# One order of one core's work set anew: fp32r groups, first loads on two queues, ScalarE's table early

## The chip, the cores and the metric

The kernel runs on one core of a Trainium2 chip. The metric is device time in microseconds. Engines: PE is TensorE, PEld its weight load, DVE VectorE, ACT ScalarE, POOL GpSimd, SP SyncE (here it only issues DMAs; SPq and ACTq are the queues of SyncE and ScalarE).

## The reference

Attention with random features (8 batches, 8 heads, 576 positions, head size 64, 128 features), whose output, 4608 tokens of 512, goes through two matrix products with a GELU between them.

```python
scale = 1.0 / np.sqrt(np.sqrt(D))
def phi(x):
    proj = np.einsum('bhsd,md->bhsm', x, omega)
    h = proj - np.sum(x * x, axis=-1, keepdims=True) / 2.0
    h = h - np.max(h, axis=-1, keepdims=True)
    return np.exp(h) / np.sqrt(m)
kv = np.einsum('bhsm,bhsd->bhmd', k_p, v)
z = np.sum(k_p, axis=2)
num = np.einsum('bhsm,bhmd->bhsd', q_p, kv)
den = np.einsum('bhsm,bhm->bhs', q_p, z)[..., None] + 1e-06
...
h = x @ w_in                                   # 512 -> 2048
g = 0.5 * h * (1.0 + erf(h * inv_sqrt2))
return g @ w_out                               # 2048 -> 512
```

## The kernel before

A unit is two heads of one batch; there are 32. Of each unit TensorE projects keys and queries on omega, ScalarE takes exponentials, TensorE multiplies keys by values (`kv`, line 769), turns the queries (`q_trans`, 798), multiplies them by the result (`num_plain`, 806) and turns the quotient back (`back`, 832). Units 0 to 7 ("plain") project in fp32, in `pair` (737: sixteen matmuls for each of keys and queries) and `shared` (744: the 64 positions at the edge that two heads share). Their maxima are `top` (749, VectorE), their exponentials `exp_tiles` (753, ScalarE). Units 8 to 31 ("split") copy their inputs to fp32r in a high and a low part (931, 936) and project them in groups of fp32r matmuls: `proj` (944, two or one of 256 columns for keys) and `proj_q` (966, two of 288 for queries).

The tokens form 18 blocks of 256. Block 0 goes through both products in fp32 (1203, 1257). The others are split in two f16 parts and use one level of a Strassen-like scheme for the first product (`sw1` and `sw2`, line 1216, 128 columns), GELU on ScalarE, and for the second product `mm2` (1264 to 1266, 512 columns). The weights come in 16 pieces of two DMAs of 512 KB (`w_load`, 545): eight of w_in first, then eight of w_out. Each is converted by ScalarE (`w_hi` 550, `w_lo` 555), VectorE (`w_shift` 558, `w_max` 567) and GpSimd (`w_round` 564); two buffers hold the pieces. When all of w_in is through, its largest value sets a scale, which TensorE helps to find (615, 621).

Nothing is scheduled by hand at the place where it is written. Each step is an `op` with an engine, a cost in microseconds, and the keys it reads and writes. A planner (`Planner.run`) walks through time with these costs: at every moment it gives each free engine, among the steps that are ready by its own account, the one with the lowest rank, and writes the instructions out in that order. `RANK` holds one number for each step, in the order in which the steps are made; for each engine the numbers are 0, 1, 2, ... without a gap, so a rank is a place on its engine. The costs reach the chip only through the order, and through filler matmuls (1421) where the planner sees TensorE idle for over 0.9 us. Two extra costs are known to it on TensorE: 0.057 us (`psw`) where a group tagged 'r' (fp32r) comes behind a step without a tag, and 0.3 where a 't' group comes behind another kind. The matmuls of both products have no tag. ScalarE pays 1.28 (`tsw`) when its table changes between exponential and GELU.

At the start SyncE issues omega (two DMAs to the two halves of the partitions, `load_om`, 508), then the first weight piece, the keys of unit 1, the queries of units 0 and 1, the second weight piece, the values of units 1 and 0. The keys of unit 0 go out on ScalarE's queue (`load_two`, 722; `load_v`, 718 for values). TensorE runs 17 warm-up matmuls (504). ScalarE's first step is `w_hi` of the first piece.

Of the kernel before, what the change touches and what calls it, by code (L numbers as in the profile page):

```python
# [8 lines left out]
F32 = mybir.dt.float32  # L9
# [26 lines left out]
RANK = (0, 3, 1, 0, 0, 4, 1, 4, 8, 0, 1, 1, 2, 2, 2, 5, 0, 5, 8, 3, 9, 4, 8, 12, 5, 23, 2, 6, 10, 11, 14, 7, 6, 15, 25, 18, 26, 22, 35, 25, 25, 3, 5,  # L36
# [187 lines left out]
class Planner:  # L224
# [45 lines left out]
    def run(self, lat, hop, alloc, put):  # L270
        for o in self.ops:
            o.due = RANK[o.id]
            o.left, o.ready, o.end, o.out = len(o.deps) + len(o.after), 0.0, None, False
        free, cand = {e: 0.0 for e in ('PE', 'ACT', 'DVE', 'POOL', 'SP')}, {e: [] for e in ('PE', 'ACT', 'DVE', 'POOL', 'SP')}
        self.tab, self.ptab, self.dma, now, n = None, None, 0.0, 0.0, 0
        port = {'DVE': 0.0, 'POOL': 0.0}

# [1182 lines left out]
```

## Time and profile before

| | |
|---|---|
| three runs | 942.03, 943.58 (median), 944.38 us |
| the profiled execution | 943.64 us |
| its span, first to last instruction | 941.5 us |
| TensorE busy | 925.3 us |
| VectorE busy | 748.5 us |
| ScalarE busy | 736.4 us |
| GpSimd busy | 486.8 us |

Times in a trace count from the span's start. The end of a matmul in the records is modelled: matmuls that follow one another overlap, so their cost is read from start to start, not from their durations. What stands under "idle before" is the time that an engine was empty ahead of an instruction, with the one that released it.

### The profile page before, as it was taken

The numbers are of one execution on the slowest core, as the hardware profiler recorded it, in microseconds if no ns is written. First come the engines' busy times: TensorE is split into PE (matmuls) and PEld (weight loads), VectorE is DVE, ScalarE is ACT, GpSimd is POOL, SyncE is SP. The second block draws the span as 40 slices with busy tenths as digits, with TensorE's granted clock in tenths as the row PEclk, the third lists the DMA queues.
The fourth block names the chain that finished last, engine by engine and source line by source line (L and its number), as shares of the span: only waits on it lengthen the run. The fifth ranks groups of instructions, "written<-read, shape, count | busy, mean of one in ns | idle before, by whom it ended". The sixth has DMA issues, their size and how long they took to land.

```text
span 941.5 us, 25835 instructions
## 1 busy us (share of the span) xinstructions
PE 925.3 (98%) x10041; PEld 702.6 (75%) x10041; DVE 748.5 (80%) x2086; ACT 736.4 (78%) x1615; POOL 486.8 (52%) x717
## 2 busy tenths in 40 slices
PE   7999999999999999999999999999999999999998
PEld 6996777777767777777777767777776777776776
DVE  3868898999999988879988999898788997643332
ACT  5998978889999787889779789977889886644343
POOL 1354655856778474775446667664657751400000
PEclk8999999999999999999999999999999999999999
DMA  8786324122422131221221332112122200000000
GB/s 241 229 248 200 115 52 133 35 80 69 117 60 88 41 99 56 63 66 56 68 80 41 88 91 77 51 53 63 52 75 63 63 2 24 13 14 23 1 24 24
DMA packets 46314, 71.46 MB, mean 76 GB/s; under 512 B 13680, under 2 KB 22256, under 8 KB 46192
## 3 DMA queue, kind: packets, MB, share of 16 engines
q1 hardware_dynamic: 46048, 69.51, 24.9%
q8 instruction: 79, 1.29, 0.6%
q14 instruction: 43, 0.35, 0.1%
q10 hardware_dynamic: 144, 0.29, 0.1%
HBM read 60.36 MB, written 9.44 MB: 74 GB/s over the span
## 4 chain that ended last, share of the span: by engine, by line
PE 82%; DVE 7%; ACT 4%; POOL 3%; DMA 2%; issue 2%; SPq 1%; POOLq 0%; ACTq 0%
PE h L1216 30%; PE acc L1264 10%; PE acc L1266 10%; PE acc L1265 10%; PE acc L1257 3%; PE at L944 2%; PE at L966 2%; PE h L1203 2%; PE at L1029 2%; PE at L816 2%; PE at L832 1%; PE h L769 1%; DMA vt<-in_v 1%; PE at L806 1%; POOL ts L1185 1%
## 5 line engine op out<-in xcount | busy, mean ns | idle before, releaser
L936 POOL TENSOR_TENSOR r<-xt,r 64x288 fp32r<-64x288 f32 (+2 forms) x216 | 165.8, 780 | 126.6 <-ACT r L931 81.2
L1216 PE MATMUL h<-xh,w 128*128 128x128 f16 x2176 | 217.4, 219 | 0.0
L1264 PE MATMUL acc<-woh,gh 128*128 128x512 f16 (+1 forms) x544 | 205.2, 377 | 0.0
L1265 PE MATMUL acc<-woh,gl 128*128 128x512 f16 (+1 forms) x544 | 204.5, 376 | 0.7 <-DVE gl L1254 0.7
L1266 PE MATMUL acc<-wol,gh 128*128 128x512 f16 (+1 forms) x544 | 204.5, 376 | 0.0
L1216 PE MATMUL h<-xl,w 128*128 128x128 f16 x1088 | 199.0, 219 | 0.0
L1216 PEld LDWEIGHTS <-w 128*128 128x128 f16 x3264 | 195.7, 98 | 4.2 <-issue 0.6
L1216 PE MATMUL h<-xh,wih 128*128 128x128 f16 x816 | 157.4, 220 | 2.7 <-DVE h L1234 1.5
L1216 PE MATMUL h<-xl,wih 128*128 128x128 f16 x816 | 156.6, 219 | 0.0
L1216 PE MATMUL h<-xh,wil 128*128 128x128 f16 x816 | 156.6, 219 | 0.0
L1254 DVE SCALAR_TENSOR_TENSOR gl<-h,bs,gh 128x512 f16<-128x512 f32 x136 | 101.0, 744 | 67.1 <-ACT gh L1251 66.3
L1216 PEld LDWEIGHTS <-wih 128*128 128x128 f16 x1632 | 139.9, 98 | 15.9 <-DVE h L1234 2.2
L1242 ACT ACTIVATE h<-h,bs 128x512 f32<-128x512 f32 x136 | 90.0, 662 | 61.8 <-PE h L1216 56.5
L1251 ACT ACTIVATE gh<-h,bs 128x512 f16<-128x512 f32 x136 | 93.5, 689 | 14.6 <-PE acc L1266 11.8
L1266 PEld LDWEIGHTS <-gh 128*128 128x128 f16 x560 | 54.7, 98 | 62.5
L931 ACT CAST r<-xt 128x256 fp32r<-128x256 f32 (+2 forms) x216 | 83.6, 408 | 14.3 <-PE at L966 9.4
L1216 PEld LDWEIGHTS <-wil 128*128 128x128 f16 x816 | 80.0, 98 | 12.0 <-issue 2.4
L1264 PEld LDWEIGHTS <-gh 128*128 128x128 f16 x560 | 54.7, 98 | 43.1
L1265 PEld LDWEIGHTS <-gl 128*128 128x128 f16 x560 | 54.9, 98 | 40.4 <-DVE gl L1254 1.0
L1223 ACT COPY g<-h 128x256 f32<-128x256 f32 x136 | 50.4, 371 | 35.1 <-PE h L1216 33.8
L1229 DVE TENSOR_TENSOR h<-h,g 128x256 f32<-128x256 f32 x136 | 58.8, 433 | 4.7
L1228 DVE TENSOR_TENSOR g<-h,g 128x128 f32<-128x128 f32 x136 | 38.5, 283 | 24.1 <-ACT g L1223 23.5
(232 smaller groups left out, 2138.9 us busy)
## 6 DMA issues: line engine op xcount, KB each, us to landing
xt<-in_qT SPq DMA_DIRECT2D x56, 288.0 KB, 3.8
xt<-in_kT SPq DMA_DIRECT2D x55, 288.0 KB, 4.2
out_x<-o SPq DMA_DIRECT2D x35, 256.0 KB, 2.0
raw<-in_w_in SPq DMA_DIRECT2D x16, 512.0 KB, 5.7
raw<-in_w_out SPq DMA_DIRECT2D x16, 512.0 KB, 4.4
w<-in_v SPq DMA_DIRECT2D x24, 320.0 KB, 3.0
vt<-in_v SPq DMA_DIRECT2D x8, 320.0 KB, 3.6
xt<-in_kT ACTq DMA_DIRECT2D x1, 288.0 KB, 3.0
```

The costliest lines, as they stand in the source:

```text
L931: nc.scalar.copy(G['r', u, x][:, 0:b - a], xf[:, a:b])
L936: nc.gpsimd.tensor_tensor(r, xf[D:, a:b], r, op=ALU.subtract)
L1216: nc.tensor.matmul(h, w[p], x[r], start=first and i + m == 0, stop=last and i == 1 and m == 2, skip_group_check=True)
L1223: nc.scalar.copy(G['sa', n, c], G['h', n, c][:, 0:2 * P])
L1228: nc.vector.tensor_tensor(q, hv[:, 3], sa[:, 0:P], op=ALU.add)
L1229: nc.vector.tensor_tensor(hv[:, 1:3], hv[:, 1:3], q.unsqueeze(1).broadcast_to([P, 2, P]), op=ALU.add)
L1242: nc.scalar.activation(h, h, AF.Gelu, scale=G['bs', n][:, 2:3])
L1251: nc.scalar.activation(G['gh', n, c], G['h', n, c], AF.Copy, scale=G['bs', n][:, 3:4])
L1254: nc.vector.scalar_tensor_tensor(G['gl', n, c], G['h', n, c], G['bs', n][:, 3:4], G['gh', n, c], op0=ALU.mult, op1=ALU.subtract)
L1264: nc.tensor.matmul(acc, gh, woh[:, f, c0:c1], start=f == 0, stop=False)
L1265: nc.tensor.matmul(acc, gl, woh[:, f, c0:c1], start=False, stop=False)
L1266: nc.tensor.matmul(acc, gh, wol[:, f, c0:c1], start=False, stop=f == NF - 1)
```

## The change

- Omega's first half goes out on ScalarE's queue, the second on SyncE's; the keys of units 0 and 1 both go out on ScalarE's queue.
- A new step `table` on ScalarE takes one exponential of one element, which brings the exponential's table in, ahead of any data.
- The matmuls of both products that have 512 columns, or belong to block 0, are tagged 'l', so that an fp32r group behind them has no extra cost in the plan.
- Costs of some twenty steps and of DMAs (1.9 us and 340 KB/us for 1.4 and 330), and the engines' start (0.7 us for 0), are other numbers in the plan.
- `RANK` is another list; one rank more, for `table`.

By the new ranks SyncE sends omega's half, queries of unit 1, the first weight piece, queries and values of unit 0, the second weight piece, values of unit 1, and pieces 3 to 7 of w_in stand one to three places earlier. ScalarE does `table`, the exponentials of unit 0's keys (eight tiles), two of unit 1's shared tiles, `w_lo` of the first piece, four of unit 1, two of unit 0's shared tiles, `w_hi` of the first piece, four of unit 1, `w_lo` of the second piece, and then the sixteen that are left of units 0 and 1. TensorE does `pair` of unit 0's and of unit 1's keys, `shared` of unit 1 and of unit 0, `pair` of unit 1's queries, then `kv` of unit 0, and after it `pair` of unit 0's queries.

```diff
@@ -33,175 +33,175 @@
-RANK = (0, 3, 1, 0, 0, 4, 1, 4, 8, 0, 1, 1, 2, 2, 2, 5, 0, 5, 8, 3, 9, 4, 8, 12, 5, 23, 2, 6, 10, 11, 14, 7, 6, 15, 25, 18, 26, 22, 35, 25, 25, 3, 5,
...
+RANK = (0, 0, 0, 0, 0, 1, 2, 1, 5, 6, 1, 3, 1, 4, 2, 4, 8, 6, 7, 13, 12, 14, 13, 6, 12, 16, 17, 2, 11, 18, 13, 20, 14, 22, 17, 25, 19, 28, 22, 33, 23,
...
@@ -271,7 +271,7 @@
-        free, cand = {e: 0.0 for e in ('PE', 'ACT', 'DVE', 'POOL', 'SP')}, {e: [] for e in ('PE', 'ACT', 'DVE', 'POOL', 'SP')}
+        free, cand = {e: 0.7 for e in ('PE', 'ACT', 'DVE', 'POOL', 'SP')}, {e: [] for e in ('PE', 'ACT', 'DVE', 'POOL', 'SP')}
@@ -287,7 +287,7 @@
-                self.dma = max(self.dma, t + o.c + 1.4) + o.size / 330e3
+                self.dma = max(self.dma, t + o.c + 1.9) + o.size / 340e3
@@ -426,6 +426,7 @@
+    pre_t = cp.tile([1, 1], F32, name="pre_t")
@@ -504,8 +505,11 @@
-        for r in range(2):
-            nc.sync.dma_start(om32[r * D:(r + 1) * D], omT)
+        for r, e in enumerate((nc.scalar, nc.sync)):
+            e.dma_start(om32[r * D:(r + 1) * D], omT)
+
+    def table():
+        nc.scalar.activation(pre_t, ones[:, 0:1], AF.Exp)
@@ -518,9 +522,10 @@
-    op('SP', 1.2, load_om, w=['om32'], size=65e3)
+    op('SP', 0.6, load_om, w=['om32'], size=300e3)
...
+    op('ACT', 0.2, table, r=['ones'], w=['table'], tab='e')
@@ -650,9 +655,9 @@
-        op('ACT', 1.08, w_hi, pc, w=[rk + ('hi',)], r=[rk])
-        op('ACT', 1.08, w_lo, pc, r=[rk], w=pc.lk if pc.l is not None else [rk + ('lo',)])
-        op('DVE', 0.64, w_shift, pc, r=[rk, rk + ('hi',)], w=bk)
+        op('ACT', 1.14, w_hi, pc, w=[rk + ('hi',)], r=[rk])
+        op('ACT', 1.2, w_lo, pc, r=[rk], w=pc.lk if pc.l is not None else [rk + ('lo',)])
+        op('DVE', 0.7, w_shift, pc, r=[rk, rk + ('hi',)], w=bk)
@@ -680,7 +685,7 @@
-        op('DVE', 0.47, a_low2, c, r=[b, sc, ('ah2', c)], w=[('al2', c)], kind='W')
+        op('DVE', 0.69, a_low2, c, r=[b, sc, ('ah2', c)], w=[('al2', c)], kind='W')
@@ -719,7 +724,7 @@
-        (nc.sync if u.k + s else nc.scalar).dma_start(u.x2[:, s], src[u.b, 2 * u.j:2 * u.j + 2].rearrange("h d s -> (h d) s"))
+        (nc.scalar if u.k < 2 and s == 0 else nc.sync).dma_start(u.x2[:, s], src[u.b, 2 * u.j:2 * u.j + 2].rearrange("h d s -> (h d) s"))
@@ -879,7 +884,7 @@
-            op('SP', 0.45 if u.k + s else 0.05, load_two, u, s, w=[('x', s, u.k % 2)], size=295e3)
+            op('SP', 0.05 if u.k < 2 and s == 0 else 0.45, load_two, u, s, w=[('x', s, u.k % 2)], size=295e3)
@@ -1072,7 +1077,7 @@
-        op('DVE', 0.25, chain_b, b, x, r=[('cm',) + k], new=[('ct', ('ct',) + k), ('cg', ('cg',) + k)])
+        op('DVE', 0.35, chain_b, b, x, r=[('cm',) + k], new=[('ct', ('ct',) + k), ('cg', ('cg',) + k)])
@@ -1089,7 +1094,7 @@
-            op('DVE', 0.8, v_max, u, r=[u.vk], w=[('vm', b)])
+            op('DVE', 0.74, v_max, u, r=[u.vk], w=[('vm', b)])
@@ -1107,7 +1112,7 @@
-                op('ACT', 0.13 + m / 1200, x_high, u, x, r=xr + ['p2'], new=[('r', rk)])
+                op('ACT', 0.11 + m / 1200, x_high, u, x, r=xr + ['p2'], new=[('r', rk)])
@@ -1127,7 +1132,7 @@
-        op('POOL', 0.23, q_max6, u, w=[nq])
+        op('POOL', 0.39, q_max6, u, w=[nq])
@@ -1136,18 +1141,18 @@
-        op('DVE', 0.88, v_b, u, r=[u.vk, ('vsc', u.b)], w=['vb'])
+        op('DVE', 1.06, v_b, u, r=[u.vk, ('vsc', u.b)], w=['vb'])
...
-            op('POOL' if X['klp'] else 'DVE', 0.25 + 0.3 * n if X['klp'] else 0.14 + 0.15 * n, k_low, u, g, r=es, w=[('kk', g)])
+            op('POOL' if X['klp'] else 'DVE', 0.25 + 0.3 * n if X['klp'] else 0.1 + 0.13 * n, k_low, u, g, r=es, w=[('kk', g)])
...
-        op('DVE', 0.3, kv_d, u, r=[('kvz', u), ('kvh', u)], new=[('kvl', ('kvl', u))])
+        op('DVE', 0.45, kv_d, u, r=[('kvz', u), ('kvh', u)], new=[('kvl', ('kvl', u))])
@@ -1298,7 +1303,7 @@
-            op('DVE', 0.24 + m / 940, block_low, n, p, r=[('bs', n), ('xh', n), ('xh', n, p)] + (ts or xr) + xt[1:] * (p > 0), w=[('xl', n, p)],
+            op('DVE', 0.31 + m / 940, block_low, n, p, r=[('bs', n), ('xh', n), ('xh', n, p)] + (ts or xr) + xt[1:] * (p > 0), w=[('xl', n, p)],
@@ -1306,7 +1311,7 @@
-                seq('m1', 'PE', (t * 4 / 2400 + .005) * (2, 1, 1)[p], mm1, n, c, p, r=[('w32', 1, c)] + xr, w=[('h', n, c)] if p else [],
+                seq('m1', 'PE', (t * 4 / 2400 + .005) * (2, 1, 1)[p], mm1, n, c, p, tab='l', r=[('w32', 1, c)] + xr, w=[('h', n, c)] if p else [],
@@ -1318,7 +1323,7 @@
-        op('POOL' if X['cp'] else 'DVE', 0.54 if X['cp'] else 0.25, comb_c, n, c, r=[('sa', n, c)], w=[hk, ('hb', n, c)], kind='F')
+        op('POOL' if X['cp'] else 'DVE', 0.54 if X['cp'] else 0.28, comb_c, n, c, r=[('sa', n, c)], w=[hk, ('hb', n, c)], kind='F')
@@ -1332,10 +1337,10 @@
-                seq('m2', 'PE', 0.86 if n < N32 else 6 * ((c1 - c0) / 2400 + .0025), mm2_plain if n < N32 else mm2, n, c, i, c0, c1, r=gr, w=[key] if c else [],
+                seq('m2', 'PE', 0.86 if n < N32 else 6 * ((c1 - c0) / 2400 + .0025), mm2_plain if n < N32 else mm2, n, c, i, c0, c1, tab='l', r=gr, w=[key] if c else [],
...
-                    op('ACT', 0.68 if n else 0.6, store, n, i, c0, c1, r=[key] + ([('bo', n), ('bs', n)] if n >= N32 else []), w=[('o', n, i)] if c0 else [],
+                    op('ACT', 0.62, store, n, i, c0, c1, r=[key] + ([('bo', n), ('bs', n)] if n >= N32 else []), w=[('o', n, i)] if c0 else [],
```

## Rows read from the trace of the kernel before

**Rows 1.** The page, busy time of each engine, share of the span, instructions.

```profile
PE 925.3 (98%) x10041; PEld 702.6 (75%) x10041; DVE 748.5 (80%) x2086; ACT 736.4 (78%) x1615; POOL 486.8 (52%) x717
```

**Rows 2.** Busy time of the engines in stretches from 15 to 800 us: the stretch, its length, then PE, PEld, DVE, ACT and POOL, the granted share of TensorE's clock, the mean busy share of the DMA engines, GB/s.

```profile
15.00:20.00 5.00, 3.06 (x19) 3.09 (x20) 1.10 (x2) 5.00 (x18) 0.61 (x1) 0.80 0.75 244
20.00:25.00 5.00, 5.00 (x32) 4.45 (x31) 2.22 (x6) 2.70 (x10) 1.93 (x2) 0.51 0.71 193
25.00:60.00 35.00, 34.71 (x353) 32.23 (x353) 28.18 (x66) 33.53 (x95) 13.24 (x10) 1.00 0.83 241
60.00:200.00 140.00, 139.48 (x1106) 102.57 (x1105) 119.48 (x247) 121.15 (x233) 85.32 (x109) 1.00 0.35 111
200.00:300.00 100.00, 97.00 (x1125) 74.35 (x1124) 94.27 (x299) 91.25 (x212) 75.20 (x109) 1.00 0.29 81
300.00:400.00 100.00, 99.67 (x1176) 76.09 (x1174) 88.52 (x275) 81.76 (x191) 59.40 (x96) 1.00 0.24 70
400.00:500.00 100.00, 100.00 (x1183) 75.94 (x1182) 85.97 (x256) 81.14 (x170) 55.58 (x83) 1.00 0.22 64
500.00:600.00 100.00, 98.94 (x1124) 74.82 (x1123) 91.84 (x281) 86.53 (x199) 65.30 (x92) 1.00 0.28 78
600.00:700.00 100.00, 99.10 (x1137) 74.37 (x1135) 87.14 (x255) 84.75 (x183) 58.44 (x93) 1.00 0.21 60
700.00:800.00 100.00, 98.79 (x1160) 74.42 (x1157) 86.22 (x255) 80.56 (x178) 57.23 (x86) 1.00 0.12 36
```

**Rows 3.** The timeline of all engines, 0 to 20 us: start, time, engine, line, instruction, tiles, how many; in brackets the idle time before it and what ended it.

```profile
0.73 0.38 ACTq L722 DMA_DIRECT2D xt<-in_kT  x1
...
0.74 1.21 SPq L508 DMA_DIRECT2D om<-in_omT  x2
...
1.05 3.64 PE L504 MATMUL h<-w 128*128 128x256 bf16 x17 [1.05 <-DVE w L495]
...
5.10 0.23 DVE L511 TENSOR_SCALAR om<-om 128x128 f32<-128x128 f32 x1 [3.49 <-DMA om<-in_omT]
...
5.38 1.16 PE L737 MATMUL at<-om,xt 64*128 64x128 f32 x16 [0.69 <-DVE om L511]
...
6.58 1.29 DVE L749 TENSOR_REDUCE nm<-at 128x4 f32<-128x512 f32 x2 [0.66 <-PE at L737]
8.51 1.28 ACT L550 ACT_TABLE_LOAD   x1 [8.51 <-DMA raw<-in_w_in]
...
9.22 0.37 PE L737 MATMUL at<-om,xt 64*128 64x128 f32 x1 [1.59 <-DMA xt<-in_kT]
...
10.83 2.16 ACT L753 ACTIVATE et<-at,nm 128x128 f32<-128x128 f32 x8
...
16.94 3.18 PE L769 MATMUL h<-vt,et 128*128 128x65 f32 x18 [2.46 <-DMA vt<-in_v]
```

**Rows 4.** The chain that ended last, followed back from the end, 0 to 75 us: its two longest pieces that are DMAs, start and time.

```profile
7.54 9.26 DMA vt<-in_v
...
52.13 6.86 DMA raw<-in_w_in
```

**Rows 5.** The timeline of TensorE around 389.5 us, where an fp32r group (L944) stands behind a 128-column matmul (L1216).

```profile
389.42 0.22 PE L1216 MATMUL h<-xh,wil 128*128 128x128 f16 x1
389.47 0.22 PE L1216 MATMUL h<-xl,wih 128*128 128x128 f16 x1
389.50 0.48 PE L944 MATMUL at<-om,r 128*128 128x256 f32 x2
389.83 0.39 PE L1264 MATMUL acc<-woh,gh 128*128 128x512 f16 x1
390.05 0.38 PE L1265 MATMUL acc<-woh,gl 128*128 128x512 f16 x1
```

**Rows 6.** The timeline of TensorE around 418 us, where such a group stands behind a 512-column matmul (L1266).

```profile
418.09 0.38 PE L1266 MATMUL acc<-wol,gh 128*128 128x512 f16 x1
418.12 0.59 PE L944 MATMUL at<-om,r 128*128 128x256 f32 x2
418.55 0.39 PE L1264 MATMUL acc<-woh,gh 128*128 128x512 f16 x1
```

**Rows 7.** DMA issues by line, in three stretches (issued in 0 to 3, in 3 to 5 and in 5 to 8 us): how many, size of each, median time from issue to landing.

```profile
xt<-in_kT ACTq DMA_DIRECT2D x1, 288.0 KB, 3.0
om<-in_omT SPq DMA_DIRECT2D x2, 32.0 KB, 3.4
...
xt<-in_kT SPq DMA_DIRECT2D x1, 288.0 KB, 6.0
...
vt<-in_v SPq DMA_DIRECT2D x2, 320.0 KB, 9.2
```

**Rows 8.** The timeline of ScalarE, 20 to 75 us.

```profile
21.01 0.58 ACT L802 COPY qh<-acc 128x512 f32<-128x512 f32 x1 [0.32 <-PE acc L798]
23.43 0.27 ACT L802 COPY qh<-h 128x128 f32<-128x128 f32 x1 [1.83 <-PE h L798]
23.59 1.15 ACT L753 ACTIVATE w<-at,nm 128x128 f32<-128x128 f32 x4
...
59.09 1.15 ACT L550 ACTIVATE raw<-raw 128x1024 f32<-128x1024 f32 x1 [1.26 <-DMA raw<-in_w_in]
```

**Rows 9.** Groups of instructions on VectorE: line, operation, tiles, shapes, count, busy time, mean ns of one, and the idle time before them.

```profile
L1011 DVE SCALAR_TENSOR_TENSOR w<-w,vsc 128x640 f16<-128x640 f32 x24 | 26.9, 1121 | 1.8 <-ACT w L1008 1.7
```

336 rows, old and new, of the table RANK are left out of this document.

## The prediction

> **What bounds the kernel now.** I read the page first [rows 1]: TensorE is busy 925.3 of 941.5 us. A faster VectorE or ScalarE is therefore worth nothing in itself; only TensorE's idle time, its clock and the spacing of its matmuls can move the end. Next the table by stretch [rows 2]. From 20 us on TensorE hardly stops: 0.29 us idle in 25 to 60, 0.52 in 60 to 200, and 3.00, 0.33, 0, 1.06, 0.90 and 1.21 in the six hundreds from 200 to 800, 6.5 us together. Its clock is granted in full, save around 20 us: 0.80 in 15 to 20 and 0.51 in 20 to 25, which is 1.0 + 2.45 = 3.4 us of full-speed time. What is left is the start, so I read it instruction by instruction [rows 3]. After the warm-up matmuls (to 4.69) TensorE does one pair of projections at 5.38, waits until 9.22 for keys, and waits again until 16.94, when the first long k-v product begins. The chain of waits [rows 4] says for what: the values of unit 0, issued at 7.54 and 9.26 us on the way. ScalarE, which makes all the exponentials, does nothing until 8.51, loads its table there (1.28 us), works on a weight piece, and starts its first exponential at 10.83, although the first maximum is there at 6.58 + 0.65 = 7.2 [rows 3]. From then on it is nearly full, 33.53 of 35 us in 25 to 60 [rows 2]. So the start is set by loads and ScalarE, the rest by TensorE.
>
> **The profiled execution** took 943.64 us, 2.15 more than its span; the three runs' median is 943.58. The sum is made against 943.6.
>
> **fp32r groups.** A run of fp32r matmuls (lines 944 and 966) behind a 128-column matmul costs 389.83 - 389.47 = 0.36 us from the start of the matmul ahead to the start of the one behind, of which 0.055 is the 128-column step itself: 0.30 for the two [rows 5]. Behind a 512-column matmul it is 418.55 - 418.09 = 0.46, of which 0.22 is that matmul's own step [rows 5, 6]: 0.24. So the change of kind costs 0.06 us, and behind 512 columns it is hidden. The new tag 'l' tells the planner so. It makes no matmul different; only the order can gain. The ranks of the diff are places, one permutation for each engine, so they can be sorted: in the trace 62 of 171 runs of fp32r stand behind 512 columns, in the new ranks 87 of 179, which leaves 92 exposed in place of 109. 17 x 0.06 = 1.0 us, all on TensorE's path. Bounds: 0, if the emitted order strays from the ranks, and 25 x 0.06 = 1.5, if the 8 runs that the ranks split off stay merged; I take 1.0.
>
> **The start: issues.** Omega's two halves went out one behind the other on SyncE (1.21 us for both), each 3.4 us to landing; VectorE waited for them until 5.10 [rows 3, 7]. Now one half goes first on ScalarE's queue, and the keys of units 0 and 1 behind it. An issue there takes 0.38 us [rows 3]; two more are 0.76 us on a ScalarE that has nothing to do until 8.51, so they cost nothing. If that cover were gone they would cost 0.76. Omega lands about 0.6 earlier; the first pair then waits for the warm-up, at 4.69, not for omega: 0.7 us sooner than 5.38.
>
> The page "DMA: Bandwidth & Descriptors" of the Trainium skill (Issuing engines are not separate DMA queues) holds that transfers issued from several engines share the same 16 DMA engines and interleave, so that a second issuer saves the issue time alone. That speaks against counting on more than the 0.6 us for omega. What is gained beyond it here must come from order, and I count it so.
>
> **The start: order of bytes.** SyncE now sends queries of unit 1, the first weight piece, queries and values of unit 0, and only then the second weight piece; before, two pieces and the other values went ahead of unit 0's values. Sizes are in [rows 7]. Values of unit 0 landed at 16.8 behind 4.0 MB; the keys of unit 1 at 9.2 behind 1.7 MB: 2.3 MB in 7.6 us, 0.30 MB/us. Now 2.62 MB stand ahead: 16.8 - 1.38/0.30 = 12.2. Keys of unit 1: 0.65 MB if ScalarE's queue is served alone, 1.25 if SyncE's gets as much, so 9.2 - 1.05/0.30 to 9.2 - 0.45/0.30, 5.7 to 7.7; I take 6.5. The first weight piece comes later, as 0.59 MB are moved ahead of it: 8.51 + 2.0 = 10.5, and unit 0's queries at 11.5.
>
> **The start: ScalarE.** The table load is moved to where the engine is idle. Then, in the order of its new ranks: eight exponentials of unit 0 (0.27 each, [rows 3]) from 4.69 + 1.16 + 0.65 + 0.1 = 6.6 to 8.8, two of unit 1 to 9.3 (its shared projections end near 8.3, some 0.6 behind 6.5 + 1.16), a wait for the weight piece to 10.5, its conversion (1.15, [rows 8]) to 11.7, four and two more to 13.3. That releases the first k-v product at 13.3 in place of 16.94. Another conversion, 4 exponentials, a conversion, 16 exponentials: 13.3 + 2.3 + 5.4 = 21.0, and some 0.3 for waits on the second piece. Before, the same exponentials were through at 23.59 + 1.15 = 24.7, with 0.32 + 1.83 us of waits for a half-speed TensorE among them [rows 8]. So the whole front moves by 3.4 us, and I take 3.5. Low end 1.3: those 2.15 us of waits come back with the clock. High end 6: the half clock's 3.4 us stay away as well, as far as ScalarE can follow.
>
> **Does it stay?** From 25 us on TensorE has no holes to swallow it, so an earlier front is an earlier end, if ScalarE and the weights follow. One wait speaks against: at 52.13 the chain goes through a weight load for 6.86 us, and ScalarE waits 1.26 us for it at 59.09 [rows 4, 8]. DMA share is 0.83 in 25 to 60, so the queue has room, and the new order sends pieces 3 to 7 one to three places earlier each. I charge nothing.
>
> **The middle.** The corrected costs and places change 774 of TensorE's 1197 steps by up to 25 places, and most of ScalarE's and VectorE's. No instruction is added or removed there. What it does to the 6.5 us of waits can't be read from before; bounds are -6.5 (every hundred like 400 to 500) and 6 x 3.0 - 6.5 = +11.5 (every one like 200 to 300). One row speaks for a gain: line 1011 takes 1.12 us in the mean [rows 9] where the plan had 0.88 and has 1.06 now. I take 0, nearest to the four hundreds from 400 on that scatter between 0 and 1.2.
>
> **Sum:** 943.6 - 3.5 - 1.0 = 939.1, -0.5%. A difference under 0.3%, 2.8 us, is about what can't be told from none.
>
> **Rivals.** (a) *The full clock stays.* The half clock (1.2 for 2.4 GHz) came at 18.0, as 0.80 in 15 to 20 is 2.0 us at half, after a TensorE that had waited 2.5 us up to 16.94 [rows 2, 3]. With shorter waits it may not come: another 2.5 to 3.4 us, less what ScalarE can't follow, 936. Against it: in my order TensorE still waits from 8.3 (after units 0's and 1's first projections) to 11.5, as long as before. "TensorE: Matmul & The Clock Gate" of the Trainium skill (What's actually happening) says that activity releases the throttle and idleness brings it, which speaks for this rival; the row shows one fall only. (b) *The gain is eaten.* Loads, not ScalarE, set the pace to 72 us: the same bytes must arrive, the weight piece of 59.09 comes no sooner, and TensorE waits there as long as it was ahead. Then 1.0 and little else: 942. For it: the chain's 6.86 us; against it: 0.83. (c) *The queues interleave badly.* Unit 0's keys share the engines with unit 1's queries and take the 6.0 us of a load in company, not 3.0 [rows 7]: landing at 7.1, first exponential at 9.0, 2.4 later than above; 941. (d) *Slower: new waits in the middle.* Groups put behind 512 columns wait for their converted keys or hold VectorE's work back; if the waits grow from 6.5 us by more than 4.5 + 2.8 = 7.3, the kernel is slower by over 0.3%. Every hundred like 200 to 300 gives 939.1 + 11.5 = 950.6; halfway, 947. For it: 774 moved steps; against it: five of six hundreds have little. (e) *The order is not what the ranks say*, as the planner drops a step that isn't ready by its own times: the 1.0 is lost, 940.
>
> **How the numbers follow.** Forecast 0.44, (a) 0.15, (b) 0.16, (c) 0.10, (d) 0.10, (e) 0.05. The range 933.5 to 944.5 leaves out most of (d) and the edges of the first three. Faster by over 0.3% (under 940.8): 0.36 of the forecast, 0.15 of (a), 0.05 of (c) and 0.04 of (e): 0.60. Within 0.3%: 0.16 of (b), 0.07 of the forecast, 0.05 of (c), 0.01 each of (e) and (d): 0.30. Slower: the rest of (d) and an edge of the forecast, 0.10.
>
> **What would show it.** Right: first exponential near 6.6 with the table load before 4, first k-v product near 13, ScalarE's exponentials of units 0 and 1 through near 21, no longer wait at 59, some 87 runs of fp32r behind 512 columns, 6 to 7 us of idle TensorE from 200 to 800. Wrong: first exponential after 8.5; TensorE idle by more than 1 us between 40 and 75; idle from 200 to 800 above 10 us.

## The result, and the profile after

The changed kernel took 949.29 us in the median of 7 executions (945.76 to 954.87), the kernel before 943.56 of 7 (941.15 to 944.38): ratio 1.0072, interval 1.0053 to 1.0092. The profiled execution took 947.78, with a span of 945.4. In the kernel after, line numbers behind 520 are 5 higher than in [rows 1 to 9]; in the experiments' kernels they are 22 higher (17 in e2).

The page of the kernel after, busy time of each engine (before: [rows 1]):

```profile
PE 927.3 (98%) x10046; PEld 703.6 (74%) x10046; DVE 749.9 (79%) x2086; ACT 733.8 (78%) x1616; POOL 485.6 (51%) x717
```

Its stretches, with the columns of [rows 2]:

```profile
15.00:20.00 5.00, 4.70 (x46) 4.14 (x44) 2.71 (x4) 5.00 (x18) 1.08 (x1) 1.00 1.13 328
20.00:25.00 5.00, 4.56 (x55) 3.84 (x53) 3.41 (x10) 3.25 (x8) 2.48 (x2) 1.00 1.03 279
25.00:60.00 35.00, 33.72 (x309) 31.16 (x310) 28.37 (x69) 34.99 (x100) 15.61 (x14) 0.95 0.84 253
60.00:200.00 140.00, 139.08 (x1150) 103.45 (x1149) 120.36 (x241) 117.06 (x227) 82.33 (x107) 1.00 0.31 102
200.00:300.00 100.00, 91.98 (x996) 67.56 (x994) 89.33 (x288) 83.84 (x197) 68.81 (x103) 0.98 0.28 81
300.00:400.00 100.00, 99.12 (x1180) 75.94 (x1178) 90.81 (x265) 81.55 (x188) 59.40 (x95) 1.00 0.21 61
...
500.00:600.00 100.00, 99.83 (x1151) 75.81 (x1149) 88.14 (x271) 84.77 (x191) 63.39 (x98) 1.00 0.26 73
600.00:700.00 100.00, 98.76 (x1168) 75.23 (x1165) 85.88 (x267) 86.38 (x191) 62.30 (x96) 1.00 0.23 66
```

Against [rows 2] one stretch stands out: 200 to 300, where TensorE's idle time went from 3.00 to 8.02 us, VectorE did 5 us and ScalarE 7 us less, and the clock was 0.98. The half clock of 15 to 25 is gone, but there is one in 25 to 60 (0.95 of 35 us: 1.7 us of full-speed time lost).

The timeline of the kernel after, all engines, 0 to 27 us, answers [rows 3 and 8]:

```profile
2.43 1.28 ACT L512 ACT_TABLE_LOAD   x1 [2.43 <-issue]
...
4.74 1.16 PE L742 MATMUL at<-om,xt 64*128 64x128 f32 x16
...
6.63 2.18 ACT L758 ACTIVATE et<-at,nm 128x128 f32<-128x128 f32 x8 [2.70 <-DVE nm L754]
...
12.10 2.17 PE L774 MATMUL at<-vt,et 128*128 128x65 f32 x18
...
18.58 1.24 ACT L758 ACTIVATE et<-acc,nm 128x128 f32<-128x128 f32 x4
...
24.70 1.10 ACT L555 ACTIVATE raw<-raw 128x1024 f32<-128x1024 f32 x1 [1.75 <-DMA raw<-in_w_in]
25.71 0.25 ACT L807 COPY qh<-acc 128x128 f32<-128x128 f32 x1
26.01 0.33 PE L803 MATMUL acc<-ident,w 128*128 128x128 f32 x1 [1.45 <-ACT qh L807]
```

First exponential at 6.63, first k-v product at 12.10, exponentials of units 0 and 1 through at 18.58 + 1.24 = 19.82: as forecast, or 1.2 us sooner. Then ScalarE's queue reaches the cast of the third piece of w_in, whose load is not there, and stands 1.75 us. Behind it in the queue are a copy that TensorE needs and the exponentials of unit 2.

To see where time goes when the order differs, I let each matmul count with the median spacing of its form in the trace of before (warm-up and filling matmuls count nothing), summed them in order, and took the time at which the same sum is reached, less that of before. In us, minus is a lead; e1 to e17 are experiments below:

```
at (before's time)   25    35    60   140   240   270   300   500   600   780
after              -6.2  -1.7  -2.6  -2.1  -2.5  +3.9  +5.9  +5.9  +5.0  +3.9
e1 start alone     -6.0  -0.5  -0.8  -1.3  -1.3  -1.3  -1.3  -1.3  -1.2  -0.8
e2 rest alone      -3.5  -3.5  -3.0   0.0  -0.3  +6.0  +8.0  +8.0  +6.9  +6.0
e3 184-273 old     -5.7  -1.2  -1.1  -0.7  +0.3  +0.4  +2.4  +2.4  +1.3  +0.3
e9                 -6.0  -3.9  -2.7  -3.3  -3.3  -3.3  -3.2  -3.3  -4.3  -5.4
e12                -6.2  -4.1  -3.0  -2.3  -2.7  +2.0  +4.0  +3.9  +2.9  +1.8
e17                -5.4  -3.3  -2.2  -1.8  -0.8  -0.8  -0.7  -0.8  -1.8  -2.9
```

The lead of 6.2 us at 25 is 1.7 at 35; 8.4 us are lost between 240 and 300; 2 come back between 500 and 780. Of the 8.4, 5.0 are idle time and 1.7 half clock (200 to 300); the rest shows in neither row. Before's own execution lost 3.4 us to half clock at 18 to 25, so a lead of 3.4 is none at full clock: e2, with the old start and no half clock there, leads by 3.5 at 25. Its stretches:

```profile
15.00:20.00 5.00, 3.37 (x34) 3.23 (x36) 1.46 (x3) 5.00 (x19) 0.54 (x1) 1.00 0.75 238
20.00:25.00 5.00, 5.00 (x51) 4.58 (x48) 3.38 (x8) 5.00 (x19) 2.01 (x2) 1.00 0.96 269
25.00:60.00 35.00, 34.41 (x335) 31.80 (x334) 29.19 (x70) 33.99 (x95) 15.49 (x14) 1.00 0.85 249
```

TensorE's waits in the kernel after, 200 to 300 us (what waited for what: us, times, longest):

```profile
PE h L837 <- DVE gl L1259: 3.1, 1, 3.1
PE acc L1270 <- DVE gl L1259: 1.3, 2, 0.9
PE h L1221 <- DVE gl L1259: 0.7, 1, 0.7
```

Where the 3.1 us stand, timeline of the three engines:

```profile
257.63 0.66 ACT L1247 ACTIVATE h<-h,bs 128x512 f32<-128x512 f32 x1
...
259.59 1.28 ACT L767 ACT_TABLE_LOAD   x1
260.89 2.13 ACT L767 ACTIVATE et<-et 128x2304 f32<-128x2304 f32 x1
263.06 0.69 ACT L1256 ACTIVATE gh<-h,bs 128x512 f16<-128x512 f32 x1
...
265.14 0.74 DVE L1259 SCALAR_TENSOR_TENSOR gl<-h,bs,gh 128x512 f16<-128x512 f32 x1
...
265.94 0.66 PE L837 MATMUL h<-ident,qh 128*128 128x128 f32 x4 [3.08 <-DVE gl L1259]
...
267.30 0.65 PE L1269 MATMUL acc<-woh,gh 128*128 128x512 f16 x1
```

The same steps in the kernel before:

```profile
255.53 0.66 ACT L1242 ACTIVATE h<-h,bs 128x512 f32<-128x512 f32 x1
...
256.86 0.71 ACT L1251 ACTIVATE gh<-h,bs 128x512 f16<-128x512 f32 x1
257.59 1.28 ACT L762 ACT_TABLE_LOAD   x1
258.88 2.13 ACT L762 ACTIVATE et<-et 128x2304 f32<-128x2304 f32 x1
...
259.13 0.74 DVE L1254 SCALAR_TENSOR_TENSOR gl<-h,bs,gh 128x512 f16<-128x512 f32 x1
```

The new order puts a unit's exponentials and their table load (3.4 us) between a gelu and the cast of its high half. The low half (`gl`), which frees the bank of `h`, comes 7.5 us behind its gelu (265.14 - 257.63) instead of 3.6, and TensorE wants that bank. The matmul at 267.30 then takes 0.65 us where its kind takes 0.39 at full clock [rows 5].

### The profile page after: what moved, and what is told of

Read it like the earlier page. It is cut to its first block, busy times and chain, and to the rows that moved or that the text cites. A ratio compares the mean times of both kernels' runs of the same rounds, so it can differ in the third digit from the quotient of the medians.

```text
span 945.4 us, 25850 instructions
## 1 busy us (share of the span) xinstructions
PE 927.3 (98%) x10046; PEld 703.6 (74%) x10046; DVE 749.9 (79%) x2086; ACT 733.8 (78%) x1616; POOL 485.6 (51%) x717
## 4 chain that ended last, share of the span: by engine, by line
PE 84%; DVE 7%; POOL 3%; ACT 2%; issue 2%; DMA 2%; SPq 0%; POOLq 0%; ACTq 0%
PE h L1221 30%; PE acc L1269 11%; PE acc L1270 11%; PE acc L1271 11%; PE acc L1262 3%; PE h L1208 3%; PE at L949 3%; PE at L971 3%; PE at L1034 2%; PE at L821 2%; PE at L837 1%; PE at L774 1%; PE at L811 1%; PE at L742 1%; DMA raw<-in_w_in 1%
## 5 line engine op out<-in xcount | busy, mean ns | idle before, releaser
L941 POOL TENSOR_TENSOR r<-xt,r 64x256 fp32r<-64x256 f32 (+2 forms) x216 | 164.3, 774 | 118.5 <-ACT r L936 90.3
L1269 PEld LDWEIGHTS <-gh 128*128 128x128 f16 x560 | 54.9, 98 | 44.2 <-ACT gh L1256 0.8
L949 PE MATMUL at<-om,r 128*128 128x256 f32 x216 | 56.1, 342 | 1.1 <-POOL r L941 0.6
```

The source lines that it names most:

```text
L941: nc.gpsimd.tensor_tensor(r, xf[D:, a:b], r, op=ALU.subtract)
L949: nc.tensor.matmul(o[:, t], r[:, t * P:(t + 1) * P], om, start=True, stop=True)
L1269: nc.tensor.matmul(acc, gh, woh[:, f, c0:c1], start=f == 0, stop=False)
```

## The experiments

Each ratio is to executions of the kernel before in the same round, and isn't the quotient of the medians. "Planned" times are those that the kernel's planner gives its steps. In a mixed order the planner takes each engine's steps strictly by their place; one order hands over to the other where both have done nearly the same steps:

```diff
-RANK = (places of the new order)
+RANK = (places of the old or the new order, by planned time)
                 for o in cand[e]:
+                    if o.due != at[e]:
+                        continue
```

**Which stretch (e1, e2, e3).** e1: new start, old order from 63 us. e2: the reverse, on the kernel before. e3: the changed kernel with the old order at 184 to 273 us.

> The changed kernel, with its own order of the steps through about the first 60 us (two queues, early table and new order there) and the order of the kernel before from there to the end. Theory M (the loss is made by the new order between 200 and 300 us, the start is a gain): the start's lead of 2 to 3 us at 60 us is kept to the end, so 940.5 to 942.5 us against 943.6 of the kernel before, and no half clock after 35 us. Rival S (the loss comes from the changed start, because everything behind it then meets its loads and its buffers at other times): 947 to 950, with the stalls of 250 to 295 us still there.

> The kernel before with its own start (one queue for omega, no early table) and its own order through about 60 us, and the changed kernel's order from there on. Theory M: the stalls of 240 to 295 us are there without the new start, so the lead of 2 to 3 us is missing and the loss of 6 to 8 us is not: 950 to 953 us. Rival S: 943 to 944, as the kernel before.

> The changed kernel with the old order put back for the steps planned between 184 and 273 us alone, where the two orders hold the same sets of steps at both ends. Theory M: the wait of TensorE of 3 us at 262.7 us and the half clock behind it go, so 941 to 944 us. Rival L (the loss is spread over the later order, from 273 us on, and what stands at 262 us is only its first place): 947 to 950. Rival S as in the first run: 947 to 950.

Measured 942.48 (ratio to before 1.0019, 0.9998 to 1.0039), 949.97 (1.0083, 1.0055 to 1.011) and 943.3 (1.0014, 0.9994 to 1.0034). The loss is the order of the middle (e2 loses 8.3 us at 240 to 300, and 3 at 60 to 140, behind the place where the two orders meet); the start neither makes it nor, by e1, gains anything to speak of.

**One place mended (e4).** In four places the high half is cast behind its gelu again:

```diff
 gelu 3,3                                  (ScalarE's queue)
+g_high 3,3
 x_high u12 ... proj_lo u12
 exps u11
-g_high 3,3
```

> The changed kernel with its order, but in four places (chunk 3 and chunk 6 of block 3, chunk 0 of block 5, chunk 4 of block 8) the high half of a gelu result is cast right behind its gelu on ScalarE, where the new order has put an exp of a unit with its table load (1.28 and 2.13 us) between the two, and the low half is moved forward on VectorE to go with it; nothing else moves. The new order has six such places, the old one two. Theory G (a narrower form of M: the h bank, which the low half releases, is held through the exp, and the next step of TensorE that wants a bank waits): the 3 us wait at 262.7, the half clock behind it and most of 284 to 291 us go: 942 to 944.5 us. Rival V (VectorE is late in this stretch whatever is put there, and another step becomes the late one): 946 to 949 with the waits at other lines.

948.44 (1.006, 1.0041 to 1.0079), against 949.29: the 3.1 us wait and the half clock behind it are gone from its trace, but other waits for VectorE and ScalarE, up to 1.3 us, came, with 2.5 us of matmuls that the planner put in to fill a hole it saw. At a granted clock of 0.996 the medians are 948.7 (4) and 948.2 (3): nothing is gained. The narrow theory falls, the rival holds.

**Upstream or on the spot (e5, e6).** RANK old at 184 to 247 us alone, or at 247 to 273 alone.

> The changed kernel with the old order of the steps planned between 184 and 247 us alone; the steps planned behind 247 us, with the place where TensorE waits 3 us, keep the new order. Theory U (upstream: TensorE's new order between 200 and 245 us takes steps of the FFN before those of the attention units 9 to 11, VectorE and ScalarE have too little to do there, and the work put off is what TensorE waits for at 250 to 270 us): most of the loss goes, 943.5 to 945.5 us, and VectorE is over 9 of 10 us busy at 210 to 230 us again. Rival P (the place itself: exp between gelu and its high half, 262 us, whatever came before): the wait stays, 947.5 to 949.5 us.

> The other half: the changed kernel with the old order of the steps planned between 247 and 273 us alone; the steps planned at 184 to 247 us keep the new order. Theory U: VectorE enters 247 us some 3 us late as before, TensorE still waits at 250 to 270 us, at other lines: 946.5 to 949 us. Rival P: 943.5 to 945.5 us.

947.78 (1.0058, 1.0039 to 1.0077) and 948.05 (1.0069, 1.0043 to 1.0095). e5 comes out as P says and e6 as U says, so neither theory holds for both: e5 keeps the wait (3.0 us, and 5 us lost at 260 to 270); e6 has lost it, and loses 5.8 us at 240 to 250 instead. The new order of either half alone costs nearly all of the loss.

**The start (e7, e8).** e7 is e1 with one cast moved; e8 has the new order again behind 307 us.

```diff
 q_copy u0,1                               (ScalarE's queue)
-w_hi w1.2
 q_copy u0,2
 exp_tiles u2
 exp_tiles u2
+w_hi w1.2
```

> The first run's kernel (new start, old order from 60 us on) with one step of ScalarE moved: the cast of the third piece of w_in stands behind the first two exps of unit 2 and the last copy of unit 0's queries, not ahead of them. Theory B (the start's lead of 4 to 6 us at 25 us is given back because ScalarE stands there 1.75 us for that piece's load, at 22.95 to 24.70 us, with the copy that TensorE waits 1.45 us for and the exps of unit 2 behind it; the idle TensorE is followed by half clock): TensorE's wait at 24.3 us goes, the lead at 40 us is 1.5 to 3 us more than the first run's, and the time 939.5 to 941.5 us where the first run had 942.5. Rival R (loads are late anyway: the next piece's cast or unit 3's data waits in its place): 942 to 943, as the first run.

> The run before with the new order again behind 307 us, so the start with its moved cast, the old order from 60 to 307 us, the new one from there. By cumulative TensorE work the changed kernel wins back 2 us between 550 and 780 us against the kernel before. Theory K (that gain is the order's own and doesn't need the loss ahead of it): 2 us under the run before, 937.5 to 939.5 us. Rival C (it is only the end of a queue that was late, so it can't be had without the loss): as the run before.

948.27 (1.0063, 1.0044 to 1.0082) and 944.78, from 938.14 to 947.29 (1.0008, 0.9984 to 1.0031). A miss that taught most. Timeline of e8:

```profile
26.87 1.21 DVE L589 TENSOR_REDUCE wmax<-w 128x1 f32<-128x1024 f32 x1
28.00 0.68 DVE L580 TENSOR_SCALAR w<-raw 128x1024 int32<-128x1024 int32 x1
...
29.01 0.49 DVE L850 TENSOR_TENSOR nx<-at,dn 128x320 f32<-128x320 f32 x1
...
29.65 0.65 PE L766 MATMUL at<-om,xt 64*64 64x128 f32 x8 [2.29 <-DVE nx L850]
```

The wait for the load is gone, and a longer one follows for unit 0's second normalisation, which stands behind two weight steps on VectorE. What comes behind it is in the stretches of e8 (columns as above):

```profile
28.00:32.00 4.00, 2.35 (x17) 2.21 (x18) 3.75 (x9) 4.00 (x15) 2.35 (x1) 0.78 0.89 291
32.00:44.00 12.00, 12.00 (x71) 11.67 (x72) 3.84 (x12) 7.70 (x17) 2.50 (x2) 0.50 0.68 210
```

Twelve us of half clock with TensorE busy throughout: 6 us lost. Of the 18 executions of e7 and e8, 14 have a granted clock of 0.991 to 0.993; three of e8's at 1.000 took 938.1 to 938.5. By granted clock, medians and counts of executions (seven at 0.995 or 0.999 are left out):

```
granted clock     1.000        0.998        0.996        0.989 to 0.993
before          940.3 (17)   942.0 (42)   944.1 (46)
after           945.8 (1)                 948.2 (3)    952.0 to 954.9 (3)
e1              941.8 (3)                 942.1 (4)    947.3 to 948.8 (4)
e8              938.2 (3)    939.7 (1)                 944.7 to 947.3 (8)
e9              938.4 (10)   940.0 (1)
e11             940.3 (1)    942.2 (4)    943.7 (4)    947.1 to 947.2 (3)
e12             945.7 (1)    947.2 (3)    948.4 (1)
e17             940.2 (9)                 943.4 (1)
```

**The second move, and the start's parts (e9, e11, e18).** e9 is e8 with the normalisation moved; e18 is e9 with the early exponential made a copy, to be without the early table; e11 has the changed kernel's table and queues, and the old order.

```diff
 norm u0,0                                 (VectorE's queue, e9)
+norm u0,1
 w_max w1.1
 w_shift w1.2
-norm u0,1
```
```diff
-        nc.scalar.activation(pre_t, ones[:, 0:1], AF.Exp)
+        nc.scalar.copy(pre_t, ones[:, 0:1])                     (e18)
```

> The kernel of the run before (start with the moved cast, old order from 60 to 307 us, new order behind) with one more step moved: on VectorE the second normalisation of unit 0 stands right behind the first, not behind the maximum over a piece of w_in and the shift of the next piece. In the two runs with the moved cast alone TensorE waited 2.3 us at 27.1 us for that normalisation (its bank), and half clock followed for 13 to 17 us; three of their executions that had no half clock took 938.1 to 938.5. Theory B2 (the start's lead is lost at whichever step stands too late there, and the half clock behind the wait multiplies it): the wait at 27 us goes, no or little half clock, 937 to 939.5 us in the median. Rival R2 (the next load or the next exp is late in its place and the clock falls all the same): 942 to 946, as the run before.

> The changed kernel's early table load and its two queues for omega and the first keys, with the order of the kernel before in everything else. Theory T (what the start gains is the table's 1.28 us and the first keys; the exps still stand behind the cast of the first piece of w_in): a lead of 1 to 2 us at 25 us, kept to the end: 940.5 to 942.5 us. Rival N (in the old order the first exp waits for the load of w_in anyway, so the table hides behind that wait and nothing is gained): within 0.5 us of the kernel before, run by run at the same granted clock.

> The fastest kernel so far (938.45; two moved steps, old order from 60 to 307 us) with the early exponential made a plain copy, so that ScalarE loads its table at the first real exponential, at 6.6 us. Theory T2 (ScalarE's start sets the start): the first product of keys and values moves back by about 1.3 us and the end by 0.5 to 1.3: 939 to 939.8. Rival L2 (loads or TensorE set it): the end within 0.3 us, 938.2 to 938.8. Rival H (the shift opens a wait and half clock follows): 941 and more.

e9: 938.45 (0.9967, 0.9955 to 0.998), faster than both kernels. Its stretches:

```profile
32.00:44.00 12.00, 11.48 (x116) 10.72 (x116) 9.68 (x24) 12.00 (x37) 4.86 (x3) 1.00 0.83 237
...
200.00:300.00 100.00, 96.97 (x1124) 74.17 (x1123) 94.65 (x296) 90.43 (x210) 75.47 (x109) 1.00 0.30 86
```

e11: 943.53 (1.0014, 0.9998 to 1.0031), at equal clock as before: table and queues alone gain nothing, rival N; three of its 12 executions, at 0.993, took 947.1 to 947.2. e18: 938.52 (0.996, 0.9945 to 0.9976). But its table is still early; its timeline of ScalarE, 0 to 9 us, has

```profile
2.44 1.28 ACT L529 ACT_TABLE_LOAD   x1 [2.44 <-issue]
3.73 0.19 ACT L529 COPY pre_t<-ones 1x1 f32<-1x1 f32 x1
7.66 1.66 ACT L775 ACTIVATE et<-at,nm 128x128 f32<-128x128 f32 x6 [3.73 <-DVE nm L771]
```

as e9 has it at 2.44: the copy brings the load just as the exponential does, and none follows at 7.66. So neither T2 nor L2 was tried as meant, and what the early table is worth by itself no run shows. What e18 does show: a first exponential at 7.66 instead of 7.00, late for its maximum (`nm`) and not for the table, moved neither the k-v product (12.29 for 12.39) nor the end.

**The middle again (e10, e12 to e17).** e10: e5 with the place at 262 mended. e12: the changed kernel with the two moves of the start alone.

> The kernel with the old order at 184 to 247 us and the new one behind, with the one place mended (chunk 3 of block 3: the high half of the gelu result cast ahead of the exp on ScalarE, the low half moved forward on VectorE). Theory PU (both halves of the stretch cost for themselves: the wait at 264.5 us is this place's, and with VectorE not late from before nothing takes its place): 943.5 to 945 us, against 947.8 without the mending. Rival Q (what TensorE lacks there is work that VectorE can't deliver earlier, whatever stands first): 946 to 948 with the wait at other lines, as the mending had it in the whole new order (948.4 against 949.3).

> The changed kernel with its own order throughout but for the two steps of the start (the cast of the third piece of w_in on ScalarE, the second normalisation of unit 0 on VectorE) that the fastest run so far moved. That run, which has the old order from 60 to 307 us, took 938.4. Theory A (two losses that add: the start's wait with the half clock behind it, and the order of 184 to 307 us): the start's part goes, the wait of 2.8 us at 262 us and its half clock stay, so 938.4 and the 7 to 8.5 us that the changed kernel loses against the kernel before between 240 and 290 us: 945.5 to 947 us, and executions above 951, which the changed kernel had, no longer occur. Rival D (the middle's waits come from the state in which the start leaves the engines): the waits at 262 and 286 us shrink, 940 to 943 us.

e10: 948.25 (1.0075, 1.0048 to 1.0102), with 2.0 us of filling matmuls; three of its six executions are at 0.991, the three at 1.000 took 945.0 to 945.7, so it decides nothing. e12: 947.15 (1.0044, 1.003 to 1.0058), theory A (0.15 over its range): the two losses add. Its stretch at full clock has the middle's idle time alone:

```profile
200.00:300.00 100.00, 91.99 (x1027) 69.00 (x1026) 90.61 (x292) 85.43 (x201) 70.52 (x106) 1.00 0.28 80
```

e13, e14 and e16 repeat e4, e6 and e10 on e12; e15 and e17 put the old order into 273 to 307 and 184 to 307 us. All five are without late filling:

```diff
-        if X['fill'] and o.idle > 0.9 and o.t > 5.0:
+        if X['fill'] and o.idle > 0.9 and 5.0 < o.t < 100.0:
```

> The run before (new order, two steps of the start moved: 947.2) with the four places mended where an exp stood between a gelu and its high half, and no filling matmuls behind 100 us. Theory G (the bank held through the exp is the loss at 262 us; the earlier mending was spoilt by 2.7 us of filling matmuls): the wait of 2.8 us and the half clock behind it go, 942.5 to 944.5 us. Rival V (VectorE can't deliver earlier): 945.5 to 947, with waits at other lines.

> The same kernel as the run before the last (new order, start mended: 947.2) with the old order for the steps planned between 247 and 273 us alone, without filling matmuls behind 100 us. Theory P (the loss is the new order of these 26 us itself): 942.5 to 944.5. Theory U (the new order at 184 to 247 us leaves VectorE late, and TensorE waits for it here whatever the order): 946 to 948, with a wait of 2 to 4 us near 250 us.

> New order with the start mended (947.2), and the old order for the steps planned between 273 and 307 us alone. Theory A2 (the waits at 284 to 294 us are this stretch's own, 2.2 us in all): 944.5 to 945.5. Rival: they are the tail of the lateness at 262 us and come back at other lines: 946.5 to 948.

> New order with the start mended, the old order for the steps planned at 184 to 247 us, the one place at 262 us mended, no filling matmuls behind 100 us. Theory G: as in the first of these runs, and what VectorE lacked is there: 942 to 944.5. Rival Q (work that VectorE can't deliver earlier): 945 to 947.

> The changed kernel with the two moved steps of the start (947.2) and the old order for the steps planned between 184 and 307 us alone. Theory W (these 123 us are the whole loss, by either half of them): 938.5 to 940 us, TensorE idle by 3 to 4.5 us at 200 to 300 us as in the kernel before. Rival X (the new order of 60 to 184 us hands over a state that costs as well): 941 to 945.

e13 947.62 (1.0051, 1.0033 to 1.0068): V, no gain from the mending; at a clock of 1.000 it is slower than e12's one execution (947.6 for 945.7). e14 947.35 (1.0051, 1.0032 to 1.007; three executions, a fourth of 5.4 ms left aside): U, a wait of 3.8 us near 250. e15 945.87 (1.004, 1.0022 to 1.0057): between the two; at a clock of 0.998 its median is 1.5 us under e12's, so most of the 2.2 us are that stretch's own. e16 945.54 (1.0027, 1.0017 to 1.0038): Q. e17 940.25 (0.998, 0.9964 to 0.9996): 6.9 us under e12, 5.5 at a clock of 1.000 (940.2 for 945.7), and 0.25 over W's range; nearly all of the loss is in these 123 us. So the filling matmuls had only stood in waits that come without them too.

What goes with most of the loss is VectorE's work before 250 us. Stretches of six kernels, columns as above: before,

```profile
200.00:250.00 50.00, 49.85 (x592) 39.29 (x591) 46.77 (x157) 45.11 (x106) 36.19 (x47) 1.00 0.35 96
250.00:270.00 20.00, 18.44 (x192) 13.16 (x191) 19.47 (x62) 17.80 (x40) 13.95 (x19) 1.00 0.28 72
```

after,

```profile
200.00:250.00 50.00, 49.33 (x535) 36.92 (x533) 44.22 (x149) 40.66 (x97) 35.11 (x44) 1.00 0.34 95
250.00:270.00 20.00, 15.19 (x167) 11.03 (x166) 19.59 (x60) 17.95 (x38) 12.76 (x17) 0.93 0.29 78
```

e13, the place mended,

```profile
200.00:250.00 50.00, 49.34 (x535) 36.96 (x532) 44.24 (x149) 40.66 (x97) 35.06 (x44) 1.00 0.32 95
250.00:270.00 20.00, 16.06 (x176) 11.53 (x173) 19.59 (x60) 17.91 (x39) 12.76 (x17) 1.00 0.30 78
```

e14, old at 247 to 273,

```profile
200.00:250.00 50.00, 45.88 (x514) 35.54 (x513) 44.24 (x147) 39.39 (x93) 35.03 (x44) 0.96 0.33 94
```

e5, old at 184 to 247,

```profile
200.00:250.00 50.00, 49.89 (x580) 38.40 (x579) 45.49 (x155) 43.73 (x98) 35.85 (x46) 1.00 0.34 96
250.00:270.00 20.00, 15.56 (x176) 12.16 (x175) 17.40 (x53) 16.33 (x39) 11.10 (x15) 0.96 0.31 78
```

and e17:

```profile
200.00:250.00 50.00, 49.83 (x604) 39.36 (x602) 47.14 (x159) 44.84 (x104) 36.02 (x46) 1.00 0.34 96
250.00:270.00 20.00, 18.43 (x192) 13.10 (x189) 19.47 (x59) 17.57 (x40) 13.94 (x18) 1.00 0.30 78
```

Third busy column: in before, after, e13 and e17 VectorE has nearly no room at 250 to 270 (19.5 of 20). Where it did 46.8 to 47.1 us in the 50 before, TensorE idles 1.6 us there; where it did 44.2, TensorE idles 4 to 5 us, there or (e14) just ahead. My reading: work that VectorE could have done at 200 to 250 and wasn't given is waited for at 250 to 270, and it doesn't matter which step is mended there. That is argued from the rows, not shown, and two things speak against it. In e5 VectorE is nearer to the old order before 250 (45.5) and has room behind (17.4 of 20), and TensorE still idles 4.4 us. And ScalarE's work before 250 falls with VectorE's (fourth column, 45.1 to 40.7), so the rows can't tell which of the two is late. No run has one engine's old order with the others' new one.

## Why the prediction was wrong

- **What bounds the kernel**: right that only TensorE's idle time and clock move the end; wrong that "what is left is the start". The waits of 200 to 300 were small in the old order, not small by nature.
- **The middle, "I take 0"**: the step that failed. Measured, where I put 0: 8.4 us lost between 240 and 300, of them 5.0 us more idle time and 1.7 us of half clock at 200 to 300; e17, with the old order there, gets 5.5 to 6.9 us back. It is rival (d), at a chance of 0.10, in one hundred rather than in all, and by other waits: of the 8.0 us idle, waits of fp32r groups for converted keys and queries make 1.2 (lines 949 and 971, 0.6 each), the low half of the gelu 5.1. The row for it stood in [rows 2]: VectorE 94.27 and ScalarE 91.25 of 100 us busy at 200 to 300, the one hundred where both are over 90; I took my value from the hundreds behind 400. The test that I named, over 10 us idle from 200 to 800, came out at 10.4.
- **The start's issues, bytes and ScalarE**: right in their mechanism, and in size right or 1.2 us too slow (first exponential 6.63 for 6.6, k-v product 12.10 for 13.3, exponentials through at 19.8 for 21.0). The Trainium skill's page "DMA: Bandwidth & Descriptors" (Issuing engines are not separate DMA queues) has a second issuer save the time of the issue alone. e11 agrees: second issuer and early table by themselves moved nothing at the end (940.25 at full clock, 940.3 before).
- **"Does it stay?"**: failed too. I looked for the swallowing wait at 59 us, where the old trace had it for the seventh piece, and charged nothing; the new order met the load of the third piece. That piece's turn on ScalarE came 7.5 us sooner than before (22.95 for 30.49), its load landed only 2.5 us sooner (24.60 for 27.07). That is rival (b)'s mechanism at another place. At a clock of 1.000 the start is worth nothing: -3.5 was 0 in e9 (a lead of 3.3 against a before that had lost 3.4 to its clock) and +1.5 in e1 (941.8 against 940.3). At 0.996 e1 is 2.0 under before (942.1 for 944.1), so the granted clock alone doesn't sort its executions. That the changed kernel leads by 2.5 us at 240, near my 3.5, is luck: the lead is the old half clock.
- **Rival (a), the clock**: what a good start does gain. e9 keeps a clock of 1.000 in 10 of 12 executions, before in 17 of 110; that and the order behind 307 us, 2 us, are e9's 4.0 (by medians). My argument against it, a TensorE that waits from 8.3 to 11.5, was wrong: projections and 19 filling matmuls stand there, and the one wait left is 0.2 us. "TensorE: Matmul & The Clock Gate" of the Trainium skill (What's actually happening) has idleness bring the half clock. e8 and e9 agree: the wait at 27 us was cut from 2.3 to 0.6 us (with one of 0.7 behind it), the clock at 32 to 44 went from 0.50 to 1.00. But the length of one wait doesn't decide it: in e2 TensorE waits 2.1 us up to its first k-v product, and the clock stays at 1.00 through 15 to 60 (rows above); in the changed kernel half clock follows a wait of 1.45. e2's wait:

```profile
16.63 2.25 PE L786 MATMUL h<-vt,et 128*128 128x65 f32 x18 [2.09 <-ACT et L770]
```

- **fp32r**: as far as the trace tells, right in mechanism and size. 87 of 179 runs stand behind 512 columns, as the ranks said. Read as in [rows 5, 6], less the step ahead, a run of one, two and four matmuls of 256 columns takes 0.12, 0.24 and 0.48 us behind 512 columns and 0.18, 0.30 and 0.53 behind 128 (medians of the kernel after): 0.12 for each matmul, and 0.06 more behind 128 columns alone. So the 0.24 is the two matmuls themselves, the 8 runs more cost nothing where they stand behind 512, and 17 exposed runs less are 1.0 us. No run tried it apart, and at the end it can't be seen: at 300 to 500, with 12 exposed runs less (0.7 us), the lag is 5.9 at both ends, but TensorE also idles 0.55 us more there (0.88 for 0.33 at 300 to 400).

Why the changed kernel scatters (945.8 to 954.9) is the start again. Of 55 executions with the changed start as it was (after, e1, e3 to e6, e10), 15 have a granted clock of 0.993 or less and took 947.3 to 954.9; of 64 with both steps moved (e9, e12 to e18) none has.

## What to carry to other kernels

When all orders are set anew, look for the stretch in which the other engines are over 90% busy: here that one hundred cost 5 to 8 us of 940, and mending the step that waited longest gained nothing (e13). When loads don't move as far as the steps, list each queue's next load and what stands behind it. Compare executions at the same granted clock before a gain at the start is believed, and look in the trace whether an experiment's edit did what it was made for (e18).

## What was not expected of the hardware

A wait of 2.3 us of TensorE at 27 us was followed by 12 us and more at half clock although TensorE was busy all the time (12.00 of 12.00 at 0.50), some 6 us lost; in e9, with 0.6 us of wait, none. Yet e2's wait of 2.1 us was followed by none, and e8 itself ran at 0.998 to 1.000 in four of 12 executions; what decides is not shown. The kernel before took 940.3 us where the granted clock was 1.000 and 944.1 where it was 0.996.

ScalarE's table load doesn't need an exponential: in e18 a plain copy brought it at 2.44 us (it took 1.28 us), and the exponentials from 7.66 us on had no other ahead of them.
